# Cosformer attention and a token-mixing layer on one core: q divided by its cosine, one tangent product in place of two products, a new order of the steps

## The chip, the cores and the metric

One core of a Trainium2 chip runs the whole program. The metric is the device time of one execution in microseconds, from the launch to the end of the last store. Three runs of the kernel before gave 117.19, 118.63 and 122.79 us, median 118.63 us. The profile is one further execution.

## The reference

`q`, `k` and `v` are (8 batches, 8 heads, 576 positions, 64) in fp32. The attention is linear, with a cosine and a sine weight for each position:

```python
theta = pi / 2 * pos / S                   # S = 576
phi(x) = concat(relu(x) * cos(theta), relu(x) * sin(theta))   # 64 -> 128 features
kv  = einsum('bhsf,bhsd->bhfd', phi(k), v)
z   = sum(phi(k), axis=s)
num = einsum('bhsf,bhfd->bhsd', phi(q), kv)
den = einsum('bhsf,bhf->bhs', phi(q), z) + 1e-06
x   = num / den                            # then (batch, 576, 8 heads * 64)
# the token-mixing layer, per batch:
wq, wk = x @ w_q, x @ w_k                  # 512 -> 64
mixed  = (wq @ wk.T / sqrt(64)) @ x
out    = relu(mixed) @ w_out               # 512 -> 512, fp32
```

The cosine and the sine belong to positions, not to features. So `num` and `den` of one position can both be multiplied or divided by any number without a change of `x`, as long as the 1e-06 is scaled too.

## The kernel before, in words

The work is cut into 16 units H, two per batch; one holds four heads as two pairs (`pr`) of two heads (`r`), 128 partitions by 2 x 576 values each of k, q and v. The program is written out by hand in the string `ORDER`: every word is one step, and the steps are issued to the engines' queues in exactly this order. Each engine works through its own queue in order. A word such as `RK4@G` names the step (RK), its index (4) and, where there is a choice, the engine: `A` ScalarE, `V` VectorE, `G` GpSimd. `:4` names the PSUM bank that the step's matmuls write; a or b behind an index is one half.

The steps of a unit H, with the lines of the profile:

- `LK`, `LQ`, `LV` (L133): two loads each, from SyncE's queue, into five buffers per tensor. `LW` loads the weights (0 and 1 the two small ones, 2 to 5 a quarter of `w_out` each).
- `RK`, `RQ` (L188 on ScalarE, L190 on GpSimd): relu of k and q to bf16. `CV` (L194 or L196): v to bf16.
- `VS`: v times cosine and times sine. On VectorE (L221) from the bf16 copy in one instruction; on GpSimd (L216) from the raw v in two. The cosine and sine tables of the v side, in two extra columns, give z.
- `KV` (L242): 36 matmuls, k against the v products. `KE` copies the sums out of PSUM.
- `QT` (L253, 18 small transposes) or `QZ` (L261, 9 larger ones): q transposed into two PSUM banks as bf16.
- `QM` (L269): VectorE multiplies the transposed q, read from PSUM, by the table `qtab` of cosine and sine. One instruction per head pair half, so two per unit, 128 x 1152 each.
- `N` (L284): numerators and denominators, two groups g per unit. `EP` (L296 on ScalarE, L298 on VectorE) adds 1e-06 to the denominators of a group, `R` (L301) takes the reciprocals, `X` (L306) multiplies.
- `XT` (L319, 10 transposes) or `XR` (L332, 20 small ones) and the copy `XE`: x transposed.

Per batch follow `WK`/`KW`, `WQ`/`QW`, `KX`/`XK` (the small matmuls and their copies), `XA`/`XB` (copies across partitions), `MX`/`ME` (mixing and relu, four per batch). `WO` (L424) is the matmul with `w_out`, 36 of them, nine per two batches; `OE` copies each result into one of 16 output buffers (its number stands after the colon) and `ST` (L434) stores it.

All banks of PSUM are one tile, `PS`; the steps give their place by number. The loads and stores share SyncE's queue, in the order of the string, and a store waits there for its `OE`.

```python
    def QM(H, ps, eng, part):
        for r in range(part.start, part.stop):
            V.tensor_mul(
                qm_b[H % NQM][:, :, r, 0:C, :],
                place["QT", H][:, r].unsqueeze(1).to_broadcast([P, 2, C, D]), qtab)
```

Of the kernel before, what the change touches and what calls it, by code (L numbers as in the profile page):

```python
# [12 lines left out]
FP32 = mybir.dt.float32  # L13
# [6 lines left out]
EPS = 1.0e-6  # L20
# [4 lines left out]
LK0a LV0a LV0b LQ0a LQ0b LK0b LQ1 LV1 LK1 LV3 LQ3 LK3 LV2 LQ2 LW1 LK2 TQ0 TW0 RK0a@A TK0 T20 TV0  # L25
RQ0a@A RQ0b@A LQ5 LQ4 CV0a@G VS0a TI0 QT0:0 CV0b@G LV5 LW0 VS0b RK0b@A LK5 LW3 LV4 LK4 LW4 LW2 LW5
TZ0 QM0a KV0:2 RQ1@A LQ6 QT1:4 RK1@G KE0@A N0:2 QM0b QM1a RQ3@G CV2@G CV1@A RQ2@G LQ7 LV7 N1:0 RK2@G
LK7 LV6 LK6 EP1@A EP0@A VS1 CV3@A KV1:6 R0 X0 X1 XR0:0 QM1b KE1@A N2:6 N3:4 QZ3:2 RQ5@G CW0@G VS3
LV8 XE0@A RK3@A LK8 KV3:0 KE3@A CV5@G RK5@G EP2@V EP3@V R1 X2 X3 QM3b QM3a VS2 CV4@G LV9 LQ8 XT1:4
N6:2 EP6@V XE1@A CW1@A QZ2:4 QM2a QM2b WK0:0 KW0@A N7:6 EP7@A R3 X6 KV2:0 KE2@A RK4@G KX0:4 RQ4@A  # L30
LQ9 LK9 LV10 LQ10 XK0@A N4:2 N5:0 X7 XT3:6 XE3@A QT4:4 CW4@G CW5@G CW2@G EP4@V WQ0:6 XB0@A EP5@V R2
# [15 lines left out]
N22:4 XK4@A XB4@G N23:2 EP23@V EP22@A R11 X22 X23 WO13:0 WO9:1 KV12:6 RK13@A OE9:15@V ST9 LK14 ST5
LV15 LQ15 OE13:10@A ST13 LK15 ST17 ST12 RQ14@G XA4@G KV13:4 MX18:2 KE12@A N25:6 EP25@V KE13@A N24:0
EP24@V R12 X25 X24 ME18@A XR11:4 WO15:2 XE11@A WK5:3 MX16:6 KW5@V OE15:13@A ME16@A RQ13@G QT13:4
QM13a QM13b MX19:0 ME19@A WQ5:2 QW5@A KX5:3 XK5@V MX17:0 ME17@A QT14:6 QM14a QM14b N26:4 XA5@A N27:2  # L50
EP27@A EP26@A R13 X26 XB5@V X27 WO19:0 OE19:14@A WO20:1 OE20:15@A WO21:0 OE21:6@A ST21 ST10 MX20:4
# [13 lines left out]
def kernel(  # L65
# [100 lines left out]
    def TW(i, ps, eng):  # L166
        nc.scalar.activation(qtab, qi, AF.Sin, bias=0.0, scale=coef)
# [331 lines left out]
```

## Time and profile before

| what | value |
|---|---|
| runs | 117.19, 118.63, 122.79 us |
| profiled execution, its own time | 117.45 us |
| its span, first to last instruction | 115.7 us |
| TensorE (PE) busy | 94.3 us |
| VectorE (DVE) busy | 89.6 us |
| ScalarE (ACT) busy | 76.3 us |
| GpSimd (POOL) busy | 66.3 us |
| moved by DMA | 39.40 MB, mean 341 GB/s |

The span leaves out 1.75 us of the profiled execution's time, which lie around the first and the last instruction. Idle time of an engine is shown with what ended it. A group of instructions is one line of the code, one operation and one shape; its columns are the count, the busy time, the mean duration of one in ns, and the idle time just before them. DMA shares are of the 16 DMA engines and can come out a little above 1.

### The profile page before, as it was taken

Reading aid. Unit: us, or ns where it says so; the run is one execution under the profiler, and the core shown is the slowest. Engines: PE = TensorE matmul, PEld = TensorE weight load, DVE = VectorE, ACT = ScalarE, POOL = GpSimd, SP = SyncE. Lnnn points to the kernel's source line nnn. Section 1 sums busy time; section 2 is a strip of 40 time slices with the busy share of each in tenths; the row PEclk is TensorE's granted clock in tenths of the full one; section 3 lists DMA queues with packets and bytes.
Section 4 is the critical chain, followed back from the end, with each engine's and each line's share of the span. In section 5 each row is a group of like instructions: output and inputs, shape, how many; then the busy total and the mean of one; then the engine's idle time right before and its main releaser. Section 6 shows DMA issues by size and latency. Waiting matters only on the chain.

```text
span 115.7 us, 5176 instructions
## 1 busy us (share of the span) xinstructions
PE 94.3 (82%) x2223; PEld 63.1 (55%) x2223; DVE 89.6 (77%) x148; ACT 76.3 (66%) x138; POOL 66.3 (57%) x64
## 2 busy tenths in 40 slices
PE   0006569786995989899999999999899899999970
PEld 0005568565683566556685667657555665553420
DVE  0064799999999889779959998997889698877420
ACT  7846656438688844588588998887755845646340
POOL 6350362681879958996999999063999710010000
PEclk9999999999999999999999999999999999999999
DMA  3999999999999999999999994779999999873974
GB/s 100 316 368 396 402 390 366 381 383 363 392 387 392 391 389 389 377 374 385 391 393 392 369 351 184 220 234 291 333 405 399 403 375 393 315 277 138 354 298 166
DMA packets 20663, 39.40 MB, mean 341 GB/s; under 512 B 3232, under 2 KB 3232, under 8 KB 20640
## 3 DMA queue, kind: packets, MB, share of 16 engines
q1 hardware_dynamic: 20640, 39.07, 92.9%
q8 instruction: 17, 0.28, 1.0%
q14 instruction: 6, 0.05, 0.1%
HBM read 29.62 MB, written 9.44 MB: 338 GB/s over the span
## 4 chain that ended last, share of the span: by engine, by line
PE 61%; DMA 26%; POOL 2%; issue 2%; SPq 2%; DVE 2%; ACT 1%; POOLq 0%; DVEq 0%; ACTq 0%
PE ps L424 29%; DMA vraw<-in_v_dram 11%; DMA kraw<-in_k_dram 10%; PE ps L242 6%; PE ps L284 6%; DMA qraw<-in_q_dram 6%; PE ps L404 4%; PE ps L354 3%; PE ps L367 3%; PE ps L332 3%; PE ps L381 3%; POOL rk L190 2%; PE ps L261 2%; SPq L133 2%; PE ps L253 1%
## 5 line engine op out<-in xcount | busy, mean ns | idle before, releaser
L424 PE MATMUL ps<-wow,mix 128*128 128x512 bf16 x144 | 35.4, 380 | 0.0
L269 DVE TENSOR_TENSOR qm<-ps,qtab 128x1152 bf16<-128x1152 bf16 x32 | 22.7, 749 | 4.4 <-PE ps L253 3.6
L306 DVE TENSOR_TENSOR x<-ps,rec 128x640 bf16<-128x640 f32 x32 | 25.1, 819 | 0.7
L216 POOL TENSOR_TENSOR v<-vraw,vtab 128x1152 bf16<-128x1152 f32 x10 | 23.5, 2374 | 0.1
L221 DVE TENSOR_TENSOR v<-vb,vtab 128x2304 bf16<-128x2304 bf16 (+1 forms) x12 | 17.2, 1437 | 6.3 <-ACT vtab L156 6.0
L194 ACT COPY o<-ps 128x512 f32<-128x512 f32 x27 | 15.7, 588 | 8.2 <-PE ps L424 7.3
L424 PEld LDWEIGHTS <-mix 128*128 128x128 bf16 x144 | 12.2, 97 | 13.4 <-issue 0.9
L190 POOL TENSOR_SCALAR rk<-kraw 128x1152 bf16<-128x1152 f32 x9 | 14.1, 1568 | 9.1 <-DMA kraw<-in_k_dram 9.0
L415 ACT ACTIVATE mix<-ps 128x576 bf16<-128x576 f32 x24 | 15.4, 654 | 3.0 <-PE ps L404 2.5
L242 PE MATMUL ps<-v,rk 64*64 64x130 bf16 x576 | 12.8, 236 | 4.0 <-POOL rk L190 3.8
L284 PE MATMUL ps<-kvs,qm 64*128 64x65 bf16 x640 | 14.3, 196 | 0.7 <-DVE qm L269 0.5
L242 PEld LDWEIGHTS <-rk 64*64 64x64 bf16 x576 | 10.3, 116 | 7.8 <-POOL rk L190 4.2
L284 PEld LDWEIGHTS <-qm 64*128 64x128 bf16 x640 | 12.7, 98 | 2.8 <-issue 1.2
L253 PE MATMUL ps<-ident,rq 64*128 64x64 bf16 x162 | 4.4, 201 | 10.6 <-ACT rq L188 9.6
L196 POOL TENSOR_SCALAR vb<-vraw 128x1152 bf16<-128x1152 f32 (+1 forms) x9 | 9.5, 1052 | 5.8 <-DMA vraw<-in_v_dram 5.5
L190 POOL TENSOR_SCALAR rq<-qraw 128x1152 bf16<-128x1152 f32 x9 | 10.3, 1147 | 4.1 <-DMA qraw<-in_q_dram 3.8
L196 POOL TENSOR_SCALAR kx<-kx 64x256 bf16<-64x256 bf16 x6 | 3.6, 602 | 15.6 <-ACT kx L194 8.5
L188 ACT ACTIVATE rq<-qraw 128x1152 bf16<-128x1152 f32 (+1 forms) x8 | 8.4, 1046 | 4.0 <-DMA qraw<-in_q_dram 3.9
L194 ACT COPY xT<-ps 128x640 f32<-128x640 f32 (+1 forms) x12 | 8.1, 672 | 3.0 <-PE ps L319 2.2
L253 PEld LDWEIGHTS <-rq 64*128 64x128 bf16 x162 | 3.6, 101 | 11.3 <-ACT rq L188 10.2
L194 ACT CAST kvs<-ps 128x260 bf16<-128x260 f32 x14 | 5.3, 379 | 6.5 <-PE ps L242 6.5
L404 PE MATMUL ps<-wq,kx 64*128 64x288 bf16 x64 | 8.6, 289 | 0.5 <-ACT o L194 0.5
(51 smaller groups left out, 121.3 us busy)
## 6 DMA issues: line engine op xcount, KB each, us to landing
kraw<-in_k_dram SPq DMA_DIRECT2D x32, 288.0 KB, 5.9
vraw<-in_v_dram SPq DMA_DIRECT2D x32, 288.0 KB, 5.9
qraw<-in_q_dram SPq DMA_DIRECT2D x32, 288.0 KB, 5.9
out_dram<-o SPq DMA_DIRECT2D x36, 256.0 KB, 3.9
wof<-in_moe_w_out_dram SPq DMA_DIRECT2D x4, 256.0 KB, 5.7
wkf<-in_moe_w_k_dram SPq DMA_DIRECT2D x1, 128.0 KB, 6.2
wqf<-in_moe_w_q_dram SPq DMA_DIRECT2D x1, 128.0 KB, 5.6
```

What stands on the lines that cost most here:

```text
L190: eng.tensor_scalar(dst, s, FMAX, 0.0, op0=ALU.min, op1=ALU.max)
L194: A.copy(dst, s)
L196: G.tensor_scalar(dst, s, 1.0, 1.0, op0=ALU.mult, op1=ALU.mult)
L216: G.tensor_tensor(v2_b[H % NV2][:, pr, :, :, 0:D], raw["v"][H % NRAW][:, pr].rearrange("p (c d) -> p c d", d=D).unsqueeze(2).to_broadcast( ...
L221: V.tensor_mul(v2_b[H % NV2][:, part, :, :, 0:D], vb_b[H % NPREP][:, part].unsqueeze(3).to_broadcast([P, n, C, 2, D]), vtab.unsqueeze(1).t ...
L242: nc.tensor.matmul(kv_v[o, r, :], rk_b[H % NPREP][a, pr, c, :], v2_b[H % NV2][a, pr, c, :, 0:D + 1], start=(c == 0), stop=(c == C - 1))
L269: V.tensor_mul(qm_b[H % NQM][:, :, r, 0:C, :], place["QT", H][:, r].unsqueeze(1).to_broadcast([P, 2, C, D]), qtab)
L284: nc.tensor.matmul(nv[:, pr, u, :], qm_b[H % NQM][a, s, r, 2 * u:2 * u + 2, :], kv_b[H % 2][a, r, s, 0:D + 1], start=(u == 0 and s == 0), ...
L306: V.tensor_tensor(x_b[b % NX][:, :, 4 * h:4 * h + 4, :].rearrange("p u (w r) d -> p r w u d", r=2)[:, r], num(place["N", g])[:, :, :, 0:D] ...
L404: nc.tensor.matmul(pair(ps)[:, t, :].bitcast(FP32)[:, 0:HS], kx_b[b % 2][a, (m // 2) ^ t, (m % 2) * P:(m % 2 + 1) * P], wq_b[b % 2][a, :], ...
L415: A.activation(dst, s, AF.Relu, scale=scale_moe)
L424: nc.tensor.matmul(o, mix_b[bp % 2][:, m, rt * P:(rt + 1) * P], wow[:, m, :], start=(m == 0), stop=(m == NDM - 1))
```

## The change

Numerator and denominator of a position are divided by its cosine. What was `[q cos, q sin]` becomes `[q, q tan]`:

- `QC`, new: ScalarE copies the transposed q from PSUM into the first half of the `qm` buffer, two bf16 values at a time as one fp32, 128 x 576.
- `QM`: one product per unit, of the transposed q with the tangent table `qtan`, 128 x 1152 for both halves together, into the second half. It is no longer split.
- `EP`: 1e-06 must be divided by the cosine too. It is now a VectorE addition of a small table `etab`, for all 32 groups; the form on ScalarE is gone.
- Tables: `TW` writes sine and cosine in fp32, `TR` takes a reciprocal of 128 x 576 fp32 values, `TT` multiplies (tangent), `TE` and `TF` make `etab`.
- All 16 `VS` are on VectorE; `VS10`, `VS11`, `VS12`, `VS14` and `VS15` were on GpSimd.
- Other steps change engine: ScalarE keeps 3 `RK` and 1 `RQ` (7 and 7 before), GpSimd has 13 and 15 (9 and 9); `CV` 5 on ScalarE and 11 on GpSimd (3 and 8). A few `ME`, `OE`, `KE`, `KW`, `XE`, `XK`, `XA`, `XB` and `CW` change places too.
- `QT` 7 and `QZ` 9 (9 and 7 before); `XR` 14 and `XT` 2 (11 and 5).
- The whole string `ORDER` is new.

```diff
-LK0a LV0a LV0b LQ0a LQ0b LK0b LQ1 LV1 LK1 LV3 LQ3 LK3 LV2 LQ2 LW1 LK2 TQ0 TW0 RK0a@A TK0 T20 TV0
-RQ0a@A RQ0b@A LQ5 LQ4 CV0a@G VS0a TI0 QT0:0 CV0b@G LV5 LW0 VS0b RK0b@A LK5 LW3 LV4 LK4 LW4 LW2 LW5
...
-X4 QW0@A X5 XR2:0 QM4b QM4a VS5 RQ6@G LQ11 LK10 QZ5:2 QM5b RQ7@G QM5a XE2@A MX3:6 XA0@A ME3@A VS4
-WQ1:0 WK1:1 KW1@A MX1:6 KV5:4 ME1@A KE5@A QW1@A CV7@G KX1:1 RK7@G LK12 XK1@A MX2:4 ME2@A N11:2
-EP11@V MX0:6 N10:0 ME0@A KV4:4 EP10@V R5 X11 XA1@A MX4:6 MX5:2 CW3@A CV6@G LV11 LQ12 KE4@A N9:4
...
+LQ0b LQ0a LV0a LK0b LV0b LK0a LQ1 LV1 LK1 LV3 LK3 LQ3 LQ2 LV2 LK2 LW0 LW2 LW1 TQ0 TW0 TK0 TV0 CV0a@A
+T20 TR0 RQ0b@G TI0 RQ0a@G LQ5 LQ4 QT0:0 QC0 CV0b@A LV5 RK0b@A TZ0 TE0 RK0a@A LK5 LV4 LK4 LW4 LW3 LW5
+TT0 VS0a VS0b TF0 KV0:2 KE0@A QM0 RQ1@G LQ6 QT1:0 QM1 RK1@G RQ3@G RQ2@G N0:2 N1:4 CV1@A EP0@V VS1
...
+VS5 RQ6@G LQ11 XE3@A XT2:0 XE2@A XA0@A QZ5:6 QC5 CV7@G QC4 RQ7@G WK1:0 XB0@V QM5 KV5:2 MX0:6 RK7@G
+KE5@A KW1@V QM4 ME0@A VS4 MX3:0 MX2:2 ME2@A WQ1:4 MX1:6 ME3@A ME1@V KX1:5 XK1@V QW1@A CV6@G LV11
+LQ12 N10:0 EP10@V N11:2 EP11@V R5 X10 KV4:6 RK6@G LK11 LV12 CW3@A CW5@A WO2:5 KE4@A XB1@A OE2:0@A
...
-    qtab = pool.tile([P, 2, C, H2], BF16, name="qtab")
+    qsc = pool.tile([P, 2, C, H2], FP32, name="qsc")
+    qtan = pool.tile([P, C, H2], BF16, name="qtan")
-    eps_t = pool.tile([P, 1], FP32, name="eps")
+    etab = pool.tile([P, SC, 1], FP32, name="etab")
...
     def TW(i, ps, eng):
-        nc.scalar.activation(qtab, qi, AF.Sin, bias=0.0, scale=coef)
+        nc.scalar.activation(qsc, qi, AF.Sin, bias=0.0, scale=coef)
+
+    def TR(i, ps, eng):
+        nc.vector.reciprocal(qsc[:, 0], qsc[:, 0])
+
+    def TT(i, ps, eng):
+        nc.vector.tensor_mul(qtan, qsc[:, 0], qsc[:, 1])
+
+    def TE(i, ps, eng):
+        nc.scalar.activation(etab[0:H2, :, 0], ki[0:H2, 0:C:2, 0], AF.Sin, bias=0.0, scale=coef)
+        nc.scalar.activation(etab[H2:P, 0:SC - 1, 0], ki[H2:P, 1:C:2, 0], AF.Sin, bias=0.0,
+                             scale=coef)
+
+    def TF(i, ps, eng):
+        nc.vector.reciprocal(etab, etab)
+        nc.vector.tensor_scalar(etab, etab, EPS, None, op0=ALU.mult)
...
-    def QM(H, ps, eng, part):
-        for r in range(part.start, part.stop):
-            V.tensor_mul(
-                qm_b[H % NQM][:, :, r, 0:C, :],
-                place["QT", H][:, r].unsqueeze(1).to_broadcast([P, 2, C, D]), qtab)
+    def QC(H, ps, eng):
+        A.copy(qm_b[H % NQM][:, 0, :, 0:C, :].bitcast(FP32), place["QT", H].bitcast(FP32))
+
+    def QM(H, ps, eng):
+        V.tensor_mul(qm_b[H % NQM][:, 1, :, 0:C, :], place["QT", H],
+                     qtan.unsqueeze(1).to_broadcast([P, 2, C, D]))
...
     def EP(g, ps, eng):
-        den = num(place["N", g])[:, :, :, D:D + 1]
-        if eng is A:
-            A.activation(rec(g), den, AF.Identity, bias=eps_t)
-        else:
-            V.tensor_scalar(rec(g), den, EPS, None, op0=ALU.add)
+        V.tensor_tensor(rec(g), num(place["N", g])[:, :, :, D:D + 1],
+                        etab.unsqueeze(1).to_broadcast([P, 2, SC, 1]), op=ALU.add)
```

In the new order 11 units issue `QC` ahead of `QM` (0, 2, 3, 4, 5, 7, 9, 10, 12, 13, 15) and 5 the other way (1, 6, 8, 11, 14). The first store ahead of later loads is `ST5`, with `LQ13`, `LV14` and `LK12` behind it; before, it was `ST11`, with `LV13` and `LK13` behind it, and `LK12` was ahead of it.

More of the change, by code (lines that the diff above doesn't have):

```diff
@@ L47 @@
[L47 to L51, printed above, removed]
@@ new lines @@
+CV2@G LV7 LQ7 QC1 CV3@A KV1:0 KE1@A N3:0 N2:6 EP1@V RK2@G LK7 LV6 LK6 R0 X0 X1 XR0:4 VS3 EP2@V EP3@V
+R1 X3 X2 RK3@A KV3:2 QZ3:0 QC3 QM3 RQ5@G QZ2:6 RQ4@G LQ9 LQ8 XR1:0 QC2 XE0@A KE3@V N6:2 CV5@G N7:4
+RK5@G XE1@A VS2 CV4@G LV9 KV2:0 RK4@G LK9 LV8 LK8 LK10 LV10 LQ10 KE2@A CW0@V QM2 WQ0:6 QW0@A N5:0
+CW4@G CW2@G CW1@V WK0:7 KW0@A EP7@V EP6@V R3 X7 N4:4 EP5@V X6 KX0:2 XR3:6 XK0@A EP4@V R2 X4 X5 QZ4:4
+VS5 RQ6@G LQ11 XE3@A XT2:0 XE2@A XA0@A QZ5:6 QC5 CV7@G QC4 RQ7@G WK1:0 XB0@V QM5 KV5:2 MX0:6 RK7@G
@@ new lines @@
+QZ9:4 QC9 WO6:6 OE6:4@A WO4:7 XR6:2 XE6@A MX9:0 QM9 VS9 ME9@A OE4:5@V WO3:6 OE3:6@A WK3:2 KW3@V
+RK9@G MX10:0 QT8:4 QM8 WQ3:3 QC8 ME10@A KX3:2 QW3@A XK3@A CV8@G VS8 KV9:4 XA3@A KE9@A WO9:3 OE9:7@A
+MX13:4 XB3@V MX15:0 ME15@V RK8@G KV8:6 ME13@A RK10@G RQ10@G KE8@A N18:2 MX14:4 ME14@A N19:0 EP19@V
+EP18@V WO12:6 CV10@A WO7:7 R9 X19 X18 N17:0 EP17@V OE7:8@A N16:4 EP16@V OE12:9@A CV11@G MX12:2
+ME12@A WO5:7 OE5:10@A ST5 LQ13 LV14 LK12 WO11:6 OE11:11@A QZ10:2 QC10 WO10:7 VS10 R8 OE10:12@A X17
+X16 QM10 KV10:0 XR9:4 RQ11@G QT11:6 QM11 XE9@A KE10@A WO13:2 VS11 RQ12@G CV12@G N21:0 QC11 OE13:13@A
@@ new lines @@
+CV15@A EP27@V N26:6 EP26@V MX22:0 ME22@A R13 X27 WO18:2 X26 OE18:5@A VS15 WO19:3 OE19:1@A MX23:0
+ME23@A RQ14@G QT14:4 QM14 RK14@G XR13:6 XE13@A QC14 WO20:3 OE20:14@V ST20 ST16 ST6 ST17 ST0 ST19
+MX21:0 ME21@A KV14:6 RK15@G KV15:4 MX20:0 KE15@V XR12:2 XE12@V KE14@A N28:6 N29:4 EP29@V EP28@V
+ME20@A RQ15@G R14 QT15:0 WO23:2 WO22:3 OE23:11@A QC15 OE22:14@A ST22 ST3 ST9 ST18 ST12 ST10 WK6:2
+QM15 X29 N31:0 N30:4 KW6@A X28 XR14:6 XE14@A WQ6:2 KX6:3 WO24:6 XK6@A XB6@G EP30@V EP31@V R15 X30
+X31 OE24:13@V ST24 ST2 ST23 ST14 QW6@A WO26:7 OE26:4@A XR15:0 XE15@V XA6@G MX25:2 ME25@A MX27:4
@@ L449, in CW @@
             cast(eng, wow[:, m, :], wo_f[:, m, :])
[L451 to L453 removed]
+    steps = {f.__name__: f for f in (KV, QT, QZ, KE, QC, QM, N, EP, R, X, XT, XR, XE, WK, KW, WQ, QW, KX, XK, XA, XB,
+                                     MX, ME, WO, OE, ST, LW, CW, TK, TV, TI, TQ, TW, TR, TT, TE, TF, T2, TZ)}
+    halves = {f.__name__: f for f in (RK, RQ, CV, VS)}
     for word in ORDER.split():
```

45 lines of the change are left out of this document (15 added, 30 removed).

## The prediction

> **What bounds the kernel now.** I read the page first, then the engines' busy time by stretches, then the chain of waits, then what TensorE waited for behind the point that the chain shows.
>
> ```profile
> span 115.7 us, 5176 instructions
> PE 94.3 (82%) x2223; PEld 63.1 (55%) x2223; DVE 89.6 (77%) x148; ACT 76.3 (66%) x138; POOL 66.3 (57%) x64
> ```
>
> The profiled execution took 117.45 us, 1.75 more than its span; my sum starts from 117.45. That is 1.0% under the median of the runs (118.63) and 0.2% above the lowest (117.19). TensorE is busiest, VectorE close behind, and neither is full over the whole span, so I go by stretches. Columns: length; busy us and instructions of PE, weight loads, DVE, ACT, POOL; clock; share of the DMA engines; GB/s.
>
> ```profile
> 6.00:36.00 30.00, 20.93 (x605) 17.13 (x605) 26.62 (x40) 18.91 (x35) 15.77 (x17) 1.00 1.05 384
> 36.18:112.06 75.88, 73.41 (x1618) 46.01 (x1618) 62.79 (x109) 51.92 (x95) 47.42 (x34) 1.00 0.93 340
> ```
>
> There are two regimes. Up to 36 us TensorE idles 30.00 - 20.93 = 9.1 us while the DMA engines are full. From 36.18 on TensorE is busy 73.41 of 75.88 us. The chain says where the one hands over to the other:
>
> ```profile
> 28.01 5.64 DMA kraw<-in_k_dram
> ...
> 33.82 2.32 POOL rk L190
> ...
> 36.18 0.75 PE ps L242 x34
> ...
> 105.88 6.16 PE ps L424 x28
> ```
>
> The DMA engines are full (1.05), the k of unit 4 lands at 28.01 + 5.64 = 33.65, GpSimd makes it bf16 (RK4), and at 36.18 KV4 starts. From there nearly everything on the chain is matmul. So the end is the time at which KV4 can start, plus the TensorE work from KV4 on, plus TensorE's waits, plus a tail of an `OE`, a store and 1.75 us. TensorE's waits from 36 us on:
>
> ```profile
> PE ps L242 <- POOL rk L190: 1.2, 1, 1.2
> PE ps L253 <- issue: 0.6, 1, 0.6
> PE ps L367 <- issue: 0.5, 1, 0.5
> PE ps L261 <- issue: 0.5, 1, 0.5
> PE ps L404 <- ACT o L194: 0.5, 1, 0.5
> PE ps L242 <- DVE x L306: 0.2, 1, 0.2
> ```
>
> The first is the end of the wait for RK4. Of the rest another engine caused only 0.5 + 0.2 = 0.7 us; 1.6 us have no releaser. VectorE is busy 62.79 of 75.88 us there, yet TensorE hardly waits for it. That is the main thing to see: the change lightens engines that TensorE rarely waits for.
>
> **The change, part by part.** The durations of the kinds it touches:
>
> ```profile
> L269 DVE TENSOR_TENSOR qm<-ps,qtab 128x1152 bf16<-128x1152 bf16 x32 | 22.7, 749 | 4.4 <-PE ps L253 3.6 <-PE ps L261 0.5
> L221 DVE TENSOR_TENSOR v<-vb,vtab 128x2304 bf16<-128x2304 bf16 x10 | 15.2, 1522 | 0.3 <-POOL vb L196 0.3
> L306 DVE TENSOR_TENSOR x<-ps,rec 128x640 bf16<-128x640 f32 x32 | 25.1, 819 | 0.7
> L301 DVE RECIPROCAL rec<-rec 128x20 f32<-128x20 f32 x16 | 4.4, 275 | 1.1 <-ACT rec L296 0.5
> L298 DVE TENSOR_SCALAR rec<-ps 128x10 f32<-128x10 f32 x22 | 3.3, 163 | 2.8 <-PE ps L284 2.6
> L296 ACT ACTIVATE rec<-ps,eps 128x10 f32<-128x10 f32 x10 | 2.5, 271 | 1.6 <-PE ps L284 1.5
> L194 ACT COPY xT<-ps 128x576 f32<-128x576 f32 x5 | 3.2, 641 | 2.2 <-PE ps L319 2.2
> L188 ACT ACTIVATE rq<-qraw 128x1152 bf16<-128x1152 f32 x6 | 7.0, 1167 | 2.5 <-DMA qraw<-in_q_dram 2.5
> L188 ACT ACTIVATE rk<-kraw 128x1152 bf16<-128x1152 f32 x6 | 7.0, 1163 | 0.2 <-DMA kraw<-in_k_dram 0.2
> L216 POOL TENSOR_TENSOR v<-vraw,vtab 128x1152 bf16<-128x1152 f32 x10 | 23.5, 2374 | 0.1
> L190 POOL TENSOR_SCALAR rk<-kraw 128x1152 bf16<-128x1152 f32 x9 | 14.1, 1568 | 9.1 <-DMA kraw<-in_k_dram 9.0
> L190 POOL TENSOR_SCALAR rq<-qraw 128x1152 bf16<-128x1152 f32 x9 | 10.3, 1147 | 4.1 <-DMA qraw<-in_q_dram 3.8
> L196 POOL TENSOR_SCALAR vb<-vraw 128x1152 bf16<-128x1152 f32 x7 | 8.1, 1160 | 3.5 <-DMA vraw<-in_v_dram 3.2
> ```
>
> *VectorE.* 32 products of 749 ns become 16 of the same shape: -12.0 us. The new product reads one stream whole and repeats the table instead of the q; no row shows that form. Its ends are half a 2304 product (0.76 us) and X's rate (819 / 640 = 1.28 ns a value, 1.47 us); I take 0.749, the same source, result and size. Five v products arrive at 1.522: +7.6. Ten EP arrive at about 0.163 (0.163 to 0.275, the reciprocal's row): +1.6. The net is -2.8 us, and none of it on the chain behind 36 us except through those 0.7 us of waits.
>
> *The tables.* TR is a reciprocal of 576 values, a length that no row has. At X's rate it takes 0.74 us. If the whole difference between L301 and L298 (0.112 us for 10 values more) were the value's own cost, it takes 0.275 + 556 x 0.0112 = 6.5 us. The nearest row is the reciprocal's, so I take 6.5. TT adds 0.74, TF 0.275 + 0.163. In front of its first v product VectorE is idle now:
>
> ```profile
> 5.98 1.94 DVE L221 TENSOR_TENSOR v<-vb,vtab 128x1152 bf16<-128x1152 bf16 x2 [5.98 <-ACT vtab L156]
> ```
>
> It waits for the v side's table, which ScalarE makes after TW's sines; so TR starts earlier than 5.98, and TR and TT push the first v product back by less than 6.5 + 0.74 = 7.2 us. What hides that: VectorE idles 30.00 - 26.62 = 3.4 us between 6 and 36, the products of units 0 to 5 take 6 x 0.749 = 4.5 us less there, and TensorE itself idles 9.1. On the path: 0; with half of that cover gone, 3 us.
>
> *ScalarE.* 16 QC at 0.641: +10.3 (the same copy by size and type; its ends are half a relu of 1152 values, 0.58, and a whole one, 1.17). Out: 4 RK, 6 RQ (-4.7, -7.0) and 10 EP (-2.7); in: 2 CV, of a relu's size and types (+2.3), and some small copies. Net about 0.
>
> *GpSimd.* Ten half products of 2.374 leave (-23.7, by busy time 23.5); 4 RK (+6.3), 6 RQ (+6.9) and 3 CV (+3.5) come, and a few small casts leave: -7 or a little more. No wait of TensorE behind KV4 was for those products, so 0 on the path.
>
> *TensorE.* Two QT become QZ, three XT become XR:
>
> ```profile
> 55.25 0.50 PE ps L261 x9
> 55.76 0.56 PE ps L319 x10
> ...
> 65.78 0.60 PE ps L332 x40
> 66.39 0.61 PE ps L253 x36
> ```
>
> By pieces of the chain a QZ is 0.50, a QT half of 0.61, an XT 0.56, an XR half of 0.60: 2 x 0.195 - 3 x 0.26 = -0.39 us, of which one XT and one QT ahead of KV4 make -0.07. So -0.3 us is behind KV4, on the path.
>
> *The moved steps.* Ahead of KV4 both orders issue the same 35 TensorE steps but for those forms, so the work from KV4 on is the same. Ahead of LK4, both send SyncE's queue the same bytes (LW2 stands where LW3 stood), and the first loads only change places among themselves. Therefore KV4 cannot start much earlier: k lands at 33.65 and takes one relu. POOL's queue ahead of RK4 gains RQ4 and the first q halves, which run in its idle time (15.77 of 30 us busy). Later LK12 goes behind ST5, a wait for OE5; six WO, two KV and more stand between WO5 and KV12 on TensorE, over 6 us, and the three loads behind ST5 should land about as fast as the chain's load of 5.64 us. I price that at 0, and at 1 us without that cover. OE22 waits for the store of OE20 in the same buffer and holds ScalarE's later copies; 0 to 1 us, taken as 0.
>
> *Added waits.* N of a unit now needs ScalarE and VectorE. What is new is that both read the same two banks. No row of before has that. Either they read at once (0.749 for both) or in turn (0.641 + 0.749 = 1.39 us, against 2 x 0.749 = 1.5 for the two halves now). I take 1.39, the row of the two halves being nearest. In eleven units the VectorE product then stands behind QC; queued behind it are the X and VS that TensorE needs next. The Trainium skill (PSUM — Partial Sum Buffer, "PSUM bank collisions raise a hardware error") says that two engines may not touch one bank in the same partitions at once, reads included, and that software has to order them. By that rule the sum holds at 1.39, and each late QC is also a VectorE stall; no run here shows it yet.
>
> *The sum.* 117.45 - 0.3 (transposes) - 0.7 (the waits for ScalarE and VectorE behind KV4) = **116.45, say 116.5 us**. RK4's own wait I leave in, for this reason:
>
> ```profile
> 30.17 1.15 POOL L190 TENSOR_SCALAR rk<-kraw 128x1152 bf16<-128x1152 f32 x1
> 33.82 2.31 POOL L190 TENSOR_SCALAR rk<-kraw 128x1152 bf16<-128x1152 f32 x1 [0.29 <-DMA kraw<-in_k_dram]
> 30.38 2.14 DVE L221 TENSOR_TENSOR v<-vb,vtab 128x2304 bf16<-128x2304 bf16 x1
> 33.78 1.34 DVE L221 TENSOR_TENSOR v<-vb,vtab 128x2304 bf16<-128x2304 bf16 x1
> ```
>
> Of a GpSimd relu and a VectorE v product that meet, the later one is stretched by about the other's length: RK4 starts 0.04 us behind the product and takes 2.31 in place of 1.15; the product at 30.38, behind the relu at 30.17, takes 2.14. CV4 releases VS4 and is followed by RK4 on its queue in both orders, so they may meet again: 1.16 us, now and after.
>
> **Rivals.** *TensorE's waits go altogether.* RK4 meets no product (-1.16), and of the 1.6 us without a releaser half goes with a looser VectorE queue (-0.8): 116.45 - 1.96 = 114.5. For it: VectorE is busy 26.62 of 30 us up to 36. Against: KV4 waits for a load.
>
> *Slower: the turns on the q banks.* Where VectorE reaches QM before ScalarE has reached QC, VectorE stands still and with it X and VS. Price 0.641 each time, with no other engine's delay counted. It decides once TensorE has run out of issued work, when QT and N stand closer than 1.39 us on it. If six of the 16 units pay: 117.45 - 0.3 + 6 x 0.641 = 121.0. For it: eleven units have this order and the second order has ScalarE wait instead. Against: other matmuls stand between nearly all QT and N.
>
> *Port turns.* Five more v products meet 13 more GpSimd instructions of relu and cast. If three meetings fall on the path, at 2.14 - 1.34 = 0.8 to 1.16 us: 117.15 + about 3 = 120.1. For it: the four rows above. Against: GpSimd as a whole has 7 us less to do. The Trainium skill (SBUF — State Buffer, "Who interferes with whom") says that a VectorE instruction with two SBUF inputs and a GpSimd one that reads SBUF block each other fully, whichever is second. The rows agree (2.31 against 1.15); by the rule every one of those five can cost up to one instruction, and it speaks against this change.
>
> *Nothing gained.* If QM costs 1.47 us in its new form, VectorE is as full as before: 117.2, within the forecast's range.
>
> **How the numbers follow.** Forecast 0.55, its own range 115.2 (RK4's 1.16 gone) to 118.0 (a load or a buffer late by 1 us, the 0.7 still there); waits gone 0.23; bank turns 0.12; port turns 0.10. The range for 8 in 10 reaches from 114.2 to 119.9. Two per cent is about what a measurement of this kernel tells from no change, 115.1 and 119.8 from 117.45. Below: most of the waits' 0.23, 0.03 of the forecast, so 0.23. Above: most of the two slower cases, 0.16. The rest, 0.61, is the same.
>
> **What would show it.** KV4 (L242) starts at 35 to 36.3 us and TensorE is busy over 96% from there on. QM is 16 x about 0.75, QC 16 x about 0.64, GpSimd 57 to 60 us, VectorE 84 to 95 by TR's length. The waits of TensorE behind KV4 sum to 2 us. I am wrong if KV4 moves by over 1.5 us, if QM or N heads TensorE's waits (bank turns), or if RK in units 11 to 15 takes over 2 us and KV waits for it (port turns).

## The result, and the profile after

The changed kernel took 125.3 us (median of four runs, 124.44 to 127.22); the kernel before, run beside it, 118.48 us (117.19 to 122.79). The ratio is 1.059, 95% interval 1.042 to 1.076: slower, where I had forecast 116.5 us and given 0.16 to slower. The time lies above my range (to 119.9) and above the slower rival's 121.0.

The profiled execution of that comparison, 127.22 us, was one with a granted clock of 0.971, so I read the rows of the changed kernel from a second profile of it, taken in the experiment e5_after_again at clock 1.00. Its span is 121.8 us, against 115.7 us before.

The stretches of e5, with KV4's start as the cut, as in the prediction (columns as there):

```profile
6.00:36.00 30.00, 18.42 (x550) 15.16 (x544) 25.22 (x42) 17.59 (x34) 18.09 (x18) 1.00 1.04 377
37.58:118.18 80.60, 74.58 (x1629) 46.54 (x1628) 62.40 (x108) 54.11 (x101) 34.81 (x31) 1.00 0.87 315
```

KV4 starts 1.40 us later (37.58, was 36.18). From there to the end of the last `WO` it takes 80.60 us, was 75.85 (36.18 to 112.03): 4.75 more. The tail is the same, so 1.40 + 4.75 = 6.15 us, the 6.1 of the spans. Of the 4.75, TensorE is busy 1.17 longer (74.58 for 73.41) and stands still 3.6 longer (6.0 for 2.4). The steps themselves are no longer: TensorE's groups behind KV4, each by itself, sum to 84.0 us, before to 84.1. They overlap less than before. Behind KV4 GpSimd has 12 us less to do than before (34.81 for 47.42) and VectorE no more (62.40 for 62.79), and none of that helps.

The groups of e5, with the page's columns (count, busy us, mean ns of one, idle time before them and what ended it):

```profile
L287 DVE TENSOR_TENSOR qm<-ps,qtan 128x1152 bf16<-128x1152 bf16 x16 | 12.0, 753 | 8.9 <-ACT qm L284 6.6 <-PE ps L269 2.3
L284 ACT COPY qm<-ps 128x576 f32<-128x576 f32 x16 | 10.2, 643 | 8.4 <-DVE qm L287 4.7 <-DVE x L320 2.5 <-PE ps L277 0.6
L237 DVE TENSOR_TENSOR v<-vb,vtab 128x2304 bf16<-128x2304 bf16 (+1 forms) x17 | 23.9, 1412 | 1.6 <-ACT vb L210 0.8 <-PE ps L258 0.4 <-POOL vb L212 0.4
L311 DVE TENSOR_TENSOR rec<-ps,etab 128x10 f32<-128x10 f32 x32 | 4.6, 163 | 2.9 <-PE ps L301 2.4 <-ACT xT L210 0.2
L171 DVE RECIPROCAL qsc<-qsc 128x576 f32<-128x576 f32 x1 | 3.8, 3754 | 3.3 <-ACT qsc L168 3.3
```

The durations are those of the sum: QM 0.753 (0.749 taken), QC 0.643 (0.641), EP 0.163 (0.163), TR 3.75 (6.5 taken, bounds 0.74 and 6.5). What the sum had not is the last column. VectorE stands in front of QM for 6.6 us until ScalarE has done QC, and ScalarE in front of QC for 4.7 us until VectorE has done QM. The waits of the two engines give the count and the longest:

```profile
DVE qm L287 <- ACT qm L284: 6.6, 5, 2.6
```

```profile
ACT qm L284 <- DVE qm L287: 4.7, 4, 2.1
```

Nine waits of 1.3 us in the mean, up to 2.6. One reading of the same banks takes 0.64 or 0.75: the waiting engine doesn't wait only for the other's read, but for whatever stands in the other's queue ahead of it. What this does to the path is plain in the chain of e5, in order of time: start, length, engine and line.

```profile
80.45 0.52 PE ps L277 x9
80.99 0.65 ACT qm L284
81.64 0.02 issue
81.67 0.77 DVE qm L287
82.44 0.04 issue
82.48 0.45 PE ps L269 x18
82.95 0.65 ACT qm L284
83.60 0.02 issue
83.62 0.76 DVE qm L287
84.38 1.28 DVE v L237 x2
85.67 2.12 issue
87.79 0.24 DVE rec L311 x2
88.03 0.70 PE ps L258 x36
```

Two units in a row: transposes (L277), QC, QM, the next unit's transposes into the banks that this set free (L269), QC, QM, and behind that QM in VectorE's queue two v products and the additions, then KV. (The 2.12 us of issue are the second v product: VectorE's own rows show the two without a break from 84.30 to 87.86.) On the chain TensorE has only 0.97 of these 7.6 us. It is busy for 6.12 us of them, mostly with other steps, and stands still for 1.5: 0.35 for QM, 0.17 for a copy of VectorE, 0.94 for the additions. The chain by engine, before and then in e5: VectorE's share goes from 2% to 25%, ScalarE's from 1% to 7%.

```profile
PE 61%; DMA 26%; POOL 2%; issue 2%; SPq 2%; DVE 2%; ACT 1%; POOLq 0%; DVEq 0%; ACTq 0%
```

```profile
PE 41%; DVE 25%; DMA 15%; ACT 7%; issue 6%; POOL 3%; SPq 1%; POOLq 0%; ACTq 0%
```

TensorE's own waits behind KV4 (e5, 37 to 122 us) are small and many, 6 us together and none over 0.9; two of the first three name QC:

```profile
PE ps L258 <- DVE rec L311: 0.9, 1, 0.9
PE ps L258 <- ACT qm L284: 0.8, 2, 0.6
PE ps L418 <- ACT qm L284: 0.8, 1, 0.8
```

### The profile page after: what moved, and what is told of

The parts are those of the page before. It is cut to its first block, busy times and chain, and to the rows that moved or that the text cites. A ratio compares the mean times of both kernels' runs of the same rounds, so it can differ in the third digit from the quotient of the medians.

```text
span 125.4 us, 5172 instructions
## 1 busy us (share of the span) xinstructions
PE 96.4 (77%) x2219; PEld 65.1 (52%) x2235; DVE 91.9 (73%) x151; ACT 77.1 (61%) x142; POOL 57.4 (46%) x63
## 4 chain that ended last, share of the span: by engine, by line
PE 41%; DVE 24%; DMA 15%; ACT 9%; issue 6%; SPq 2%; POOL 1%; POOLq 0%; ACTq 0%
PE ps L438 19%; DMA vraw<-in_v_dram 10%; DVE x L320 7%; DVE v L237 6%; DVE qm L287 6%; PE ps L301 5%; DMA kraw<-in_k_dram 4%; ACT qm L284 4%; PE ps L381 3%; PE ps L258 3%; PE ps L346 3%; PE ps L368 2%; PE ps L418 2%; SPq L133 2%; ACT xT L210 1%
## 5 line engine op out<-in xcount | busy, mean ns | idle before, releaser
L206 POOL TENSOR_SCALAR rq<-qraw 128x1152 bf16<-128x1152 f32 (+1 forms) x16 | 19.1, 1192 | 16.2 <-DMA qraw<-in_q_dram 14.5
L206 POOL TENSOR_SCALAR rk<-kraw 128x1152 bf16<-128x1152 f32 x13 | 18.5, 1422 | 16.4 <-DMA kraw<-in_k_dram 13.6
L237 DVE TENSOR_TENSOR v<-vb,vtab 128x2304 bf16<-128x2304 bf16 (+1 forms) x17 | 25.0, 1474 | 0.9 <-POOL vb L212 0.4
L210 ACT COPY o<-ps 128x512 f32<-128x512 f32 x25 | 14.6, 587 | 10.0 <-PE ps L438 9.9
L438 PEld LDWEIGHTS <-mix 128*128 128x128 bf16 x144 | 12.7, 98 | 14.8 <-issue 2.1
L287 DVE TENSOR_TENSOR qm<-ps,qtan 128x1152 bf16<-128x1152 bf16 x16 | 12.0, 753 | 10.6 <-ACT qm L284 8.4
L284 ACT COPY qm<-ps 128x576 f32<-128x576 f32 x16 | 10.2, 642 | 9.2 <-DVE qm L287 5.3
L212 POOL TENSOR_SCALAR vb<-vraw 128x1152 bf16<-128x1152 f32 x11 | 12.6, 1151 | 5.7 <-DMA vraw<-in_v_dram 4.6
L214 DVE COPY o<-ps 128x512 f32<-128x512 f32 x11 | 7.6, 688 | 3.0 <-PE ps L438 2.3
L311 DVE TENSOR_TENSOR rec<-ps,etab 128x10 f32<-128x10 f32 x32 | 4.5, 162 | 5.5 <-PE ps L301 5.1
L269 PE MATMUL ps<-ident,rq 64*128 64x64 bf16 x126 | 3.5, 203 | 6.2 <-POOL rq L206 5.8
L210 ACT CAST vb<-vraw 128x1152 bf16<-128x1152 f32 (+1 forms) x6 | 6.0, 992 | 2.9 <-DMA vraw<-in_v_dram 2.9
```

The lines of the kernel that those rows point to most:

```text
L206: eng.tensor_scalar(dst, s, FMAX, 0.0, op0=ALU.min, op1=ALU.max)
L210: A.copy(dst, s)
L212: G.tensor_scalar(dst, s, 1.0, 1.0, op0=ALU.mult, op1=ALU.mult)
L237: V.tensor_mul(v2_b[H % NV2][:, part, :, :, 0:D], vb_b[H % NPREP][:, part].unsqueeze(3).to_broadcast([P, n, C, 2, D]), vtab.unsqueeze(1).t ...
L284: A.copy(qm_b[H % NQM][:, 0, :, 0:C, :].bitcast(FP32), place["QT", H].bitcast(FP32))
L287: V.tensor_mul(qm_b[H % NQM][:, 1, :, 0:C, :], place["QT", H], qtan.unsqueeze(1).to_broadcast([P, 2, C, D]))
```

## The experiments

Theory at first: the turns on the q banks are the loss. Rivals: VectorE is too full with five more v products (port turns), the loads that now stand behind stores, the new order by itself. A new theory came up when these were in: the ten additions of 1e-06 (`EP`) that moved from ScalarE to VectorE. Ratios are to the kernel before, run beside each on the same chip, with 95% intervals.

**e5_after_again** is the changed kernel once more, with no edit.

> The changed kernel once more, beside the next three on one chip, for a same-chip time and a second profile. Every theory: 1.04 to 1.08 of the kernel before. Bank turns: VectorE again waits 6 us or more for QC, and KV4 starts behind 37.5 us. A gap of TensorE without a releaser near 79 us that is a chance of one execution goes; one that belongs to the order stays.

124.39 us (123.59 to 125.05), 1.053 (1.043 to 1.064). It is the base for all that follows.

### The turns taken away

**e1_qc_from_sbuf and e6_qc_from_table**: QC reads SBUF instead of the banks, in e1 the untransposed q, in e6 a table.

```diff
-        A.copy(qm_b[H % NQM][:, 0, :, 0:C, :].bitcast(FP32), place["QT", H].bitcast(FP32))
+        A.copy(qm_b[H % NQM][:, 0, :, 0:C, :].bitcast(FP32),                              # e1
+               rq_b[H % NPREP].rearrange("p c r d -> p r c d").bitcast(FP32))
+               vtab.rearrange("p c r d -> p r c d").bitcast(FP32))                        # e6
```

> QC copies as many values of the untransposed q from SBUF instead of the transposed q from PSUM, so the first half of qm is filled with other values; order, engines and instruction counts are those of the changed kernel (124.4 us). Only the sharing of the q banks by ScalarE and VectorE is gone, and QC no longer waits for the transposes. Bank turns: the lost time comes back, 117 to 119.5 us, and VectorE waits no more for QC. Order and late loads: 122 us or more. Port turns: 124 us, unchanged.

> The changed kernel, QC copying as many values from a table in SBUF that is ready early: the first half of qm holds table values. No bank is shared and QC waits for nothing but its own buffer, so the wait for q that the first try brought in is gone. Bank turns: the stretch from KV4 to the end falls from 83 to 76 or 77 us and the whole to 1.00 to 1.03 of before. Order and late loads: still 1.04 or more. Port turns: still 1.05 or more.

e1 took 127.21 us (124.79 to 127.93) and tells nothing about the turns: the copy now waited for the q itself.

```profile
ACT qm L284 <- POOL rq L206: 12.8, 2, 7.2
```

e6, without that wait: 121.67 us, 1.027 (1.018 to 1.036). The waits between QM and QC are gone, and 2.7 us with them, half of the loss of 5.8 us. (QC doesn't wait for the transposes any more either, so the 2.7 us are the turns together with that.) KV4 starts at 37.62, as in e5; the gain lies behind it (78.72 us to the end of the last `WO` for 80.60).

**e2_old_order, e7_old_order_table, e8_old_order_qc_on_v**: the new arithmetic in the order of before. QC and QM stand where the first half of QM stood and all EP are on VectorE; e7 takes the turns away with the table, e8 with QC as a copy on VectorE.

```diff
-QM0a KV0:2 RQ1@A LQ6 QT1:4 RK1@G KE0@A N0:2 QM0b QM1a
+QC0 QM0 KV0:2 RQ1@A LQ6 QT1:4 RK1@G KE0@A N0:2 QC1 QM1
...
-EP1@A EP0@A VS1
+EP1@V EP0@V VS1
```

> The order of before (v products of units 10, 11, 12, 14 and 15 on GpSimd, loads and stores as before) with the new arithmetic: QC and QM stand where the first half product stood, the additions of 1e-06 are all on VectorE, the tables are made ahead of the first v product. Bank turns: they come with the arithmetic, in any order, 119.5 to 122 us. Order and late loads: the new arithmetic alone costs nothing, 117 to 119 us. Port turns: the five v products are back on GpSimd, 117 to 119 us.

> The old order with the new arithmetic, QC copying from the table in SBUF: first half of qm filled with table values. Against the same with QC from PSUM (1.033 of before). Bank turns: 0.98 to 1.00 of before, VectorE's waits for QC (15.4 us, 13 times) gone. If the tangent tables, EP on VectorE or ScalarE's load are what costs: still 1.02 or more.

> The old order with the new arithmetic, QC as a VectorE copy ahead of QM, so both readers of the q banks stand in one queue. VectorE has some 0.7 us a unit more than with QC on ScalarE, about what it has in the kernel before. Bank turns: 0.99 to 1.01 of before, better than with QC on ScalarE although VectorE does more. If VectorE's load decided: slower than with QC on ScalarE, 1.04 or more.

e2: 124.72 us, 1.033 (1.015 to 1.052). The turns are even longer there:

```profile
DVE qm L287 <- ACT qm L284: 15.4, 13, 3.1
```

e7: 121.67 us, 1.026 (1.013 to 1.039); e8: 121.61 us, 1.020 (1.012 to 1.027). In e8 VectorE is busy 97.8 us, 9.8 more than in e7, and the kernel is no slower for it. But 2 to 2.6% stay in the order of before although nothing waits on the banks any more. So the turns are not the whole loss, and neither is the new order.

### Rivals that fell

**e3_old_products**: the products and tables of before in the new order, with EP and all v products on VectorE as there; **e4_v_on_g**: the changed kernel with five v products back on GpSimd.

```diff
-QC2 ... QM2                                   # e3, in before.py with the new order
+QM2
-CV10@A ... VS10                               # e4, also 11, 12, 14, 15
+VS10@G
```

> The new order with the old arithmetic: QM is two products of 128 x 1152 on VectorE, no QC, no tangent tables. All v products stay on VectorE, which so has 12 us more than in the changed kernel. Bank turns: no bank is shared, so 118 to 121 us in spite of the fuller VectorE. Order and late loads: 124 us or more. Port turns: 124 us or more.

> The changed kernel with the v products of units 10, 11, 12, 14 and 15 back on GpSimd, from the raw v, and without their five casts. Port turns: 119 to 121 us. Bank turns: 123.5 to 125 us, no gain. Order and late loads: 124 to 126 us.

e3: 125.06 us, 1.044 (1.034 to 1.055): the new order is slow with the old products too. It has two products per unit again, so VectorE is busy 99.1 us, and this doesn't price the order alone. e4: 129.63 us, 1.086 (1.073 to 1.098). This run can't single out port turns, because with the five back GpSimd is full and the rest comes later. What speaks against port turns by those five is the sign that the prediction named: in e5 GpSimd's relus of k of units 12 to 15 take 1.15 to 1.29 us, not over 2, and VectorE's v products 1.499 us in the mean, no longer than the 1.522 of before.

```profile
64.00:80.00 16.00, 15.54 (x354) 9.52 (x352) 9.92 (x21) 11.05 (x22) 16.00 (x10) 1.00 0.69 230
```

**e9_early_loads and e10_early_table**: each load from unit 11 on stands directly behind the step that frees its buffer, ahead of the first store; e10 takes the turns away too.

```diff
-ST5 LQ13 LV14 LK12 ... ST13 LV13 LK13
+LK12 ... LQ13 ... LV14 ... LV13 ... LK13 ... ST5 ... ST13
```

> The changed kernel (1.053 of before on the last chip) with every load from unit 11 on issued directly behind the step that frees its buffer, ahead of the first store; nothing else moves. Late loads: 1.02 to 1.04, and the DMA engines' gap at 62 to 70 us (5 to 125 GB/s) is gone. Bank turns alone: the gap is gone and the time stays at 1.045 to 1.06. Port turns alone: stays.

> Both at once: the early loads, and QC copying from the table in SBUF (half of qm holds table values), 1.027 without the early loads. If late loads are the rest of the loss: 0.99 to 1.01. If not, as without them: 1.02 to 1.03, and the rest lies in the order itself and in port turns around KV4.

e9: 126.08 us, 1.062 (1.053 to 1.071); e10: 122.75 us, 1.035 (1.024 to 1.046). No gain: the DMA engines' idle stretch only moves. In e9 they move 387 GB/s between 64 and 80 us, and then:

```profile
80.00:96.00 16.00, 13.09 (x337) 8.90 (x335) 12.66 (x23) 12.30 (x25) 5.72 (x6) 1.00 0.28 105
```

**e11_before_small and e12_before_small_early**: the kernel before with every QZ as QT and every XT as XR; e12 with early loads besides. By the prediction's pieces that takes 7 x 0.195 + 5 x 0.26 = 2.7 us of TensorE's time away, for 113 transposes more. It was to test the premise that TensorE's work from KV4 on sets the end.

```diff
-QZ3:2 ... XT1:4
+QT3:2 ... XR1:4
```

> The kernel before with all transposes in the small form: seven QZ become QT, five XT become XR. By the chain's pieces TensorE has 7 x 0.195 + 5 x 0.26 = 2.7 us less, 2.2 of it behind KV4. If TensorE's work behind KV4 sets the end, as the prediction said: 0.980 to 0.99 of before. If VectorE and ScalarE set it as much: 0.995 to 1.005.

> The same, and every load from unit 11 on directly behind the step that frees its buffer, as in the early loads of the changed kernel. Before has a dip of the DMA engines at 70 to 80 us (184 to 234 GB/s). If loads are late there: 0.005 to 0.015 below the small transposes alone. If TensorE alone sets the end: no difference over 0.005.

e11: 123.1 us, 1.033 (1.017 to 1.048); e12: 125.99 us, 1.058 (1.044 to 1.072). The kernel got slower, but this doesn't settle the premise, because TensorE did not get its time back: behind KV4 it is busy 73.16 us for 73.41, with 16 matmuls missing from that trace and a granted clock of 0.72 between 42 and 48 us. In front of matmuls of N (L284 there) TensorE stands still with nothing named that would release it, a wait that the profile of before doesn't list:

```profile
PE ps L284 <- issue: 3.9, 3, 1.9
```

The changed kernel has only 12 matmuls more than the kernel before (2235 and 2223), so their number is hardly its loss; but it shows how little it takes to lose a few per cent here.

### The additions

**e16_before_ep_v**: the kernel before, with one thing moved: the ten EP of ScalarE are on VectorE.

```diff
-EP1@A EP0@A VS1 ... N15:4 EP15@A VS6
+EP1@V EP0@V VS1 ... N15:4 EP15@V VS6
```

> The kernel before with one part of the change alone: the ten additions of 1e-06 that ScalarE does are done by VectorE. Theory that the order of before has no slack left for VectorE (the new arithmetic in that order lost 2% even without turns): 1.005 to 1.02 with waits of TensorE for the reciprocals. Rival that the copy QC and the tables, not these additions, cost those 2%: 0.995 to 1.005.

121.68 us, 1.024 (1.015 to 1.033). Ten instructions of 0.16 us, 1.6 us of VectorE's time, cost 2.9 us (121.68 - 121.68 / 1.024). Its profiled execution shows two causes. That one has a span 4.9 us longer than the profile of before (120.6 and 115.7), so what follows are pieces of 4.9 us.

The first is the queue. VectorE's rows around VS6, before and then in e16 (start, length; in brackets the idle time before it and what ended it), show it:

```profile
45.47 1.36 DVE L221 TENSOR_TENSOR v<-vb,vtab 128x2304 bf16<-128x2304 bf16 x1 [0.28 <-POOL vb L196]
47.38 0.17 DVE L298 TENSOR_SCALAR rec<-ps 128x10 f32<-128x10 f32 x1 [0.55 <-PE ps L284]
...
48.10 1.55 DVE L306 TENSOR_TENSOR x<-ps,rec 128x640 bf16<-128x640 f32 x2
```

```profile
48.69 0.17 DVE L298 TENSOR_SCALAR rec<-ps 128x10 f32<-128x10 f32 x1 [1.62 <-PE ps L284]
48.77 1.50 DVE L221 TENSOR_TENSOR v<-vb,vtab 128x2304 bf16<-128x2304 bf16 x1
50.20 0.15 DVE L298 TENSOR_SCALAR rec<-ps 128x10 f32<-128x10 f32 x1
50.39 0.28 DVE L301 RECIPROCAL rec<-rec 128x20 f32<-128x20 f32 x1
50.70 1.56 DVE L306 TENSOR_TENSOR x<-ps,rec 128x640 bf16<-128x640 f32 x2
```

In the order the word EP15 stands ahead of VS6. As long as ScalarE did it, VectorE went past it: VS6 ran at 45.47, while TensorE was still at N. With EP15 in VectorE's own queue, VectorE stands 1.62 us in front of it until N is done, VS6 starts only behind it, and EP14, R7 and X behind VS6. Counted from the KV ahead of it (KV7, 45.10 and 46.72), X starts 3.00 us later before and 3.98 in e16. From here the chain of e16 runs on through VectorE (v product, reciprocal, X, the next v product), and KV8 starts 2.3 us later than before (55.88, was 53.56). Of these, 1.6 us are older than KV7. EP1 and EP0 stand ahead of VS1 in the same way: there X starts at 16.06 (before 14.60), and KV4 at 37.44 (before 36.18). That the one leads to the other is argued, not shown.

The second is a meeting on the way from KV9 to KV10, which takes 8.83 us (60.16 to 68.99), before 7.00 (57.84 to 64.84). There VectorE copies 64 x 256 values (XB3), behind EP17, which was ScalarE's, and EP16. The copy and GpSimd's v products, before:

```profile
62.60 0.28 DVE L198 COPY kx<-kx 64x256 bf16<-64x256 bf16 x1
62.78 9.41 POOL L216 TENSOR_TENSOR v<-vraw,vtab 128x1152 bf16<-128x1152 f32 x4
```

The same in e16, with the matmul of MX that needs the copy:

```profile
64.99 2.05 DVE L198 COPY kx<-kx 64x256 bf16<-64x256 bf16 x1
64.60 4.68 POOL L216 TENSOR_TENSOR v<-vraw,vtab 128x1152 bf16<-128x1152 f32 x2
67.10 0.29 PE L404 MATMUL ps<-wq,kx 64*128 64x288 bf16 x2 [1.51 <-DVE kx L198]
```

Before, the copy began 0.18 us ahead of GpSimd's products and took 0.28. In e16 it began 0.39 behind them, took 2.05, and TensorE stood still for 1.51, its longest wait behind KV4. Counted from KV9, GpSimd's products come 0.50 us earlier than before and the copy 0.07 later. All versions in the order of before with every EP on VectorE have this wait: 1.6 us in e2, 1.2 in e7, 1.5 in e8. In e8 it is most of the loss: KV9 starts at 57.92, 0.08 us later than before, and KV10 at 66.76, 1.92 later.

**e17_table_ep_back and e18_old_order_table_ep_back**: both causes taken away, QC from the table and the ten EP on ScalarE in their old form, in the new order and in that of before.

```diff
-EP1@V ... EP7@V
+EP1@A ... EP7@A
...
+        if eng is A:
+            A.activation(rec(g), den, AF.Identity, bias=eps_t)
```

> The changed kernel in its new order without the turns (QC copies a table from SBUF, so half of the q operand holds table values) and with the additions of 1e-06 in the form of before, the same ten of 32 on ScalarE (the constant is then not divided by the cosine). If turns (2.7 us) and additions (2.9 us) are the loss and add up: 0.99 to 1.01 of before. If the new order by itself is what costs the 2.7% that the run without turns still lost, with its later start of KV4 and the gaps of TensorE: 1.02 to 1.03 again. Between them, the additions cost less where ScalarE also has QC to do.

> The same two things taken away in the order of before: QC from a table, additions of 1e-06 as before, one product per unit; half of the q operand holds table values and the constant is not divided by the cosine. If the additions are what cost the 2.6% that this order still lost without turns: 0.99 to 1.005, and KV4 starts at 36 to 36.5 us. If the tables at the start, the copies or the number of instructions cost it: 1.015 to 1.03 again.

e18: 121.07 us (118.97 to 122.26) beside 121.25 us of the kernel before (119.26 to 124.25); the runs of both spread too widely for an interval, but the lowest of each, 118.97 and 119.26 us, agree to 0.3%. The first of these is its profiled execution: KV4 starts at 36.29, as before, and XB3's copy takes 0.42 us without a wait of TensorE. In the order of before the turns and the additions are the whole loss, as near as these runs can tell; a rest of a per cent would not show in them. e17: 126.15 us, 1.056 (1.048 to 1.064), as slow as the changed kernel. There it is the other way round: the reciprocals now wait for ScalarE.

```profile
DVE rec L321 <- ACT rec L316: 9.8, 5, 2.9
```

The new order was laid out with these additions on VectorE; ScalarE comes to them up to 2.9 us late.

### Ways out in the new order

**e13_copies_back**: e6 with nine small copies on their engines of before. **e14_qc_on_v**: QC on VectorE. **e15_crosswise**: each unit in two halves by bank, ScalarE on the one bank while VectorE is on the other.

```diff
-XB0@V KW1@V ME1@V XK1@V XA1@V KE3@V CW0@V CW1@V CW5@A          # e13
+XB0@A KW1@A ME1@A XK1@A XA1@A KE3@A CW0@G CW1@A CW5@G
-        A.copy(qm_b[...], place["QT", H].bitcast(FP32))         # e14
+        V.tensor_copy(qm_b[...], place["QT", H].bitcast(FP32))
+        src, dst, _, _ = half(H, t)                             # e15, t = 0 at the
+        A.copy(dst.bitcast(FP32), src.bitcast(FP32))            # first word, then 1
+        src, _, dst, tab = half(H, 1 - t)
+        V.tensor_mul(dst, src, tab)
```

> The changed kernel with QC copying a table from SBUF in place of the transposed q (so half of the q operand holds table values; no turns on the q banks), as in the run before of that form, and besides with nine small copies ahead of unit 7 (KE3, XB0, KW1, ME1, XK1, XA1 and three CW) on the engine that before.py has for them, ScalarE or GpSimd instead of VectorE or ScalarE. Theory that VectorE's queue ahead of unit 4's v product is what is late in the new order (XB0 took 1.05 us there beside a GpSimd relu, KW1 0.48): KV4 starts at 36.0 to 36.8 instead of 37.6 us, and the time falls from 1.027 to 1.010 to 1.018 of before. Rival that the rest lies behind KV4 (fixed gaps of TensorE, its half clock, waits spread over the second half): KV4 moves by less than 0.5 us or the gain is lost later, ratio 1.022 to 1.032.

> The changed kernel with all 16 QC as copies on VectorE, so that one engine alone reads the q banks; VectorE gets some 7 to 10 us more, ScalarE 10 us less. Theory that turns between two engines are half of the loss: although VectorE is fuller than in any version, 1.025 to 1.04 of before, against 1.053 of the changed kernel. Rival that VectorE's total work sets the end in this order: 92 + 8 = 100 us busy, 1.06 or more.

> The changed kernel with each unit but the first in two halves by PSUM bank: ScalarE copies the one bank while VectorE multiplies the other, then they change over; transposed q of the QZ form is laid out in two banks for that (chunks 0 to 4 and 5 to 8). Theory of the turns: where both engines come at about the same time a unit takes some 0.8 us instead of 1.4, but there are 15 more instructions of about 0.1 us fixed time on each engine and both engines still wait once for each other, so a gain of 0 to 2 us: 1.035 to 1.053 of before. Rival that the waiting for the other engine's arrival and not the length of the turns is what costs: 1.05 or more, slower than the changed kernel.

e13 failed: 132.09 us, 1.108 (1.095 to 1.120), because my edit sent the cast of a weight (CW0) to GpSimd, behind relus that wait for loads. So it tells nothing about the copies.

```profile
PE ps L382 <- POOL wqw L212: 9.5, 1, 9.5
```

e14: 129.45 us, 1.091 (1.078 to 1.104), as the rival said: in this order VectorE, busy 101.9 us, can't take the copies that it took without loss in the order of before (e8). e15: 124.44 us, 1.047 (1.039 to 1.055). It is not told apart from the changed kernel; the halves cost more in all (QM 14.0 us for 12.0, QC 12.7 for 10.2). Their waits for each other fall from 11.3 to 4.4 us, but QC's for the transposes grow from 1.0 to 7.4 and QM's from 2.3 to 5.2. So the sum of these waits doesn't tell what the turns cost; taking them away does (e6). No version that I ran beats the kernel before.

## Why the prediction was wrong, step by step

**Right.** The durations of QM, QC and EP; TR between its bounds and hidden; GpSimd's busy time (58.1 us; 57 to 60); loads behind ST5 not the cause (e9).

**Step that failed first: the added waits at 0.** I wrote "I take 1.39, the row of the two halves being nearest" and let nothing of it reach the path. The two do take turns: in the five profiles where both read the same banks whole (the changed kernel's two, e2, e4, e9) QC and QM of one unit never overlap, and the chain shows 0.65 + 0.77 one behind the other. The Trainium skill (PSUM — Partial Sum Buffer, "PSUM bank collisions raise a hardware error") says that two engines have to be ordered on a bank, reads included. The traces show them ordered, with 6.6 and 4.7 us of waits; what would happen without, no run here shows. My price per turn was wrong: a unit's 1.39 is right only if both engines are there. They are not, and the late one is late by its own queue, 1.3 us in the mean and up to 2.6. The whole came to 2.7 us in the new order (e5 against e6) and to 0.9 to 1.6 in that of before (1.033 against 1.026 and 1.020; these intervals overlap). The slower rival had the mechanism, with 0.641 each "with no other engine's delay counted"; the other engine's delay was the larger part.

**Second: the ten additions at 0.** I wrote "Ten EP arrive at about 0.163", and of VectorE's sum "none of it on the chain behind 36 us". The duration was right. But an EP waits for N, and all that stands behind it in VectorE's queue waits with it; and with the steps shifted, a copy falls behind a GpSimd product and holds TensorE for 1.5 us. Together this is 2.9 us in the kernel before (e16). What is queued behind the waiting instruction I had named for QM, and not for EP. Meetings with GpSimd I had priced in the rival of the port turns, but for the five v products and not for a copy.

**Behind both: the reading of the profile.** "The change lightens engines that TensorE rarely waits for" took few waits as slack. TensorE waited 0.7 us for the others because their results were there in time; it did not show how much later each could come. XB3's copy had 0.18 us to spare. From KV4 to the end the sum was TensorE's work, 0.3 us less of it, and no wait for another engine; instead TensorE's busy time grew by 1.17 us and its idle time by 3.6. The signs that I had named say the same: TensorE is busy 92.5% from KV4 on (74.58 of 80.60), not over 96, and waits 6 us, not 2.

**KV4 by the load of k4.** "KV4 cannot start much earlier" held, but it can start later: RK4 is done at 34.50 + 1.15 = 35.65 in e5, and KV4 starts at 37.58. It is TensorE's queue ahead of it that is late:

```profile
33.25 0.72 PE L258 MATMUL ps<-v,rk 64*64 64x130 bf16 x36 [0.52 <-POOL rk L206]
...
37.58 0.72 PE L258 MATMUL ps<-v,rk 64*64 64x130 bf16 x36
```

KV5 starts 0.67 us later than before (33.25, was 32.58). From KV5 to KV4 it then takes 4.33 us, was 3.60: TensorE has 3.74 us of steps in between, was 2.35 with a wait of 1.25 for RK4. So the new order has moved 1.4 us of steps from ahead of KV5 to behind it, and the load of k4 no longer decides. Unit 5's relu, for which KV5 waits 0.52 us, is done 1.9 us later than before (33.19 for 31.32).

Of those 1.9 us, 0.9 are one meeting: the relu begins behind a v product and lasts 2.04 for 1.15. XB0, the copy that follows on VectorE and stood on ScalarE before, pays for it in turn (1.05). GpSimd's row, then VectorE's:

```profile
31.15 2.04 POOL L206 TENSOR_SCALAR rk<-kraw 128x1152 bf16<-128x1152 f32 x1 [0.36 <-DMA kraw<-in_k_dram]
```

```profile
30.83 1.36 DVE L237 TENSOR_TENSOR v<-vb,vtab 128x2304 bf16<-128x2304 bf16 x1 [0.38 <-POOL vb L212]
32.22 1.05 DVE L214 COPY kx<-kx 64x256 bf16<-64x256 bf16 x1
```

The Trainium skill (SBUF — State Buffer, "Who interferes with whom") names copies on VectorE among the instructions that can take the pair of ports shared with GpSimd; these rows agree. TensorE's wait for this relu is 0.52 us, so the meeting can make at most that much of the 1.40 by which KV4 is late; the run that was to test it (e13) failed.

**What stays open.** In the new order without turns 2.7% remain (e6). In the order of before the additions explain what remained there; in the new one they can't be taken back without a new loss (e17), so I can't say what share is theirs and what share the order's. A part is in view: in e6, at one place in the middle of N22, TensorE stands still for 2.26 us with no releaser, and works at a granted clock of 0.58 for the next four.

```profile
75.10 0.61 PE L302 MATMUL ps<-kvs,qm 64*128 64x65 bf16 x28
77.97 0.36 PE L302 MATMUL ps<-kvs,qm 64*128 64x65 bf16 x12 [2.26 <-issue]
```

```profile
77.90:82.00 4.10, 4.04 (x51) 2.33 (x51) 2.00 (x4) 1.92 (x4) 3.15 (x3) 0.58 1.05 399
```

At the same place the first profile of the changed kernel has 1.96 us and e5 0.31. What the gap is, no run here shows.

## What to carry to other kernels

Before an instruction moves to another engine, write down what it waits for and what then stands behind it in that engine's queue: ten additions of 0.16 us cost 2.9 us, because v products that had been done ahead now stood behind a wait, and because a copy that had begun 0.18 us ahead of a GpSimd product now began behind it. An operation that is split between two engines on the same PSUM banks pays each engine's lateness to the other, 1.3 us a time here, not the length of one read. Few waits in a profile of a tightly ordered kernel don't mean that there is room: look how long each result lies ready before it is used, and which instructions of VectorE and GpSimd nearly meet. Busy totals say nothing of it.

## What the runs showed of the hardware

- A VectorE reciprocal of 128 x 576 fp32 takes 3.75 us, 6.5 ns a value, five times the 1.28 of X; the short ones (128 x 20) take 0.28 us.
- The tangent product, which reads q from PSUM and repeats a bf16 table, costs 0.753 us, as much as the product that repeats the q and reads a table once (0.749).
- Small copies of VectorE meet GpSimd's instructions as its products do: a copy of 64 x 256 took 1.05 us in e5 behind the start of a relu on GpSimd, and 2.05 in e16 behind that of a v product; the quickest of that shape took 0.22.
- After a gap of TensorE of 2.26 us (e6) its granted clock was 0.58 for 4.1 us, after one of 1.96 (the first profile of the changed kernel) 0.57 for 4.0, and after one of 0.31 at the same place (e5) 1.00. By the granted clock the stop in e6 cost another 4.1 x (1 - 0.58) = 1.7 us of TensorE's time, an estimate.
- A gap of TensorE without a releaser stood at the same instruction in three profiles, with lengths of 0.31 to 2.26 us, and such gaps came up in front of N when 113 transposes were added (e11).
